# The first tile's loads split by heads on two queues, with filling transposes and weight conversions planned later

## The chip, the cores and the metric

The kernel runs on one core of a Trainium2 chip, in one launch. The metric is the device time of an execution in microseconds (us), and lower is better. The engines are TensorE (PE in the profile), VectorE (DVE), ScalarE (ACT), GpSimd (POOL) and SyncE (SP), which issues transfers.

## What is computed

Windowed causal attention with a linear bias by distance, then a mixer with a token part and a channel part, then a normalized channel part. Shapes: 4 batches, 8 heads, 576 positions, head size 64, so 2304 rows of 512.

```python
scores = q @ k.T / 8 + slope * -|i - j|, only where 0 <= i - j < 128
x = softmax(scores) @ v                          # rows of 512 (8 heads x 64)
u = x + (relu(x.T @ w_tok1) @ w_tok2).T          # w_tok1: 576 x 256
x = u + relu(u @ w_ch1) @ w_ch2                  # 512 x 1536, 1536 x 512
xn = (x - mean(x)) / sqrt(var(x) + 1e-6) * g_ln
out = x + relu(xn @ w2_ch1) @ w2_ch2             # 512 x 2048, 2048 x 512
```

q, k, v are given in f32. The weights arrive as 8-byte floats, which the kernel converts itself.

## The kernel before

The rows are cut into 18 tiles of 128 positions, over all batches. In the attention, each tile's scores are made in two groups of four heads (c = 0 and 1, L592), against the keys of the tile itself and of the tile before. A group goes through VectorE (L637: bias and minimum), ScalarE (L646: exp and sum), a transpose on TensorE (L653), a copy on ScalarE and masks on GpSimd (L361, L663); then the values (L608) and `normalize` (L667) give 128 rows of `u`. The token part (`tok1`, L694, and `tok2`, L722) runs beside the attention of later tiles. After the attention come two layers of channel products. In each, a first group of 8 row tiles, a group of 2 and a second group of 8 go through steps of 256 hidden columns: first products into the tiles b (L993 to L995) and, one step later, second products into acc (L1048 to L1050), added to `u` by VectorE (L1053).

Weights are read by `load_f64` (L381). One row of 8-byte floats is loaded twice, as the halves `rh` (one buffer) and `rw` (two buffers). ScalarE makes `e` from `rh` (L416), VectorE makes `s` (L419, L421), `m` (L423) and the f32 value, `y` or `w` (L431). Matrices used in products are then split into a high and a low part, on ScalarE and on GpSimd or VectorE (L374). Inside `attention()` there are 21 such loads: five of `wt1` and four of `wt2` (the token weights) and twelve of channel weights, of which six go to the `w` buffers and six to DRAM for later (`stage_w`). The other weights are loaded while the channel layers run.

The program's order isn't that of the code. Each operation is recorded with `op`: its costs by engine, what it reads and writes. `Plan.ranks` (L189) gives each a due time, counted back from its readers through waiting times (`LAT`) and twice the costs; a buffer that is used again links its old operations to the new ones. `Plan.order` (L205) then runs a list schedule in which all transfers are one engine, "DMA", and an engine that is free takes the ready operation that is due first. The instructions are written out in the order of the planned starts, and each engine and each queue works them off in that order. All transfers are issued by SyncE, but for the three of `shift_wt1` (L543).

At the start, ten pairs of transposes of the identity (`spin`, L757) keep TensorE busy (WARM = 10). Tile 0 is loaded as one transfer of keys (L532), one of q (L534, through L353) and one of its bias table (L767), each 256 KB. The two groups of tile 0's scores are chained: nothing is put between them, and the first waits for what both need.

Of the kernel before, what the change touches and what calls it, by code (L numbers as in the profile page):

```python
# [23 lines left out]
B, H, S, D = 4, 8, 576, 64  # L24
P = 128
DM = H * D
# [6 lines left out]
RING = 4  # L33
# [9 lines left out]
X_SHIFT, STAGE_SHIFT = -20, -20  # L43

STAGE_RATES = {(0, 2): 2, (1, 0): 2}
WARM, WARM_NS = 10, 320
WT_SHIFT, WT_START, WT_STEP, SHIFT_AT, W_START, W_STEP = 0, 2, 1, 7, 12, 2
SIGN16, EXP16 = 0x80008000 - (1 << 32), 0x7F807F80


# [52 lines left out]
class Plan:  # L103
# [11 lines left out]
    HOLD_ANY = False  # L115
    AHEAD = 2000
    SPARE = {"DVE": 1200, "ACT": 0}
    LAT = {"PE": 400, "DVE": 260, "ACT": 290, "POOL": 180, "DMA": 4000, "CTL": 0}

    def __init__(self):  # L120
        self.pools, self.ops, self.rings, self.ctl = {}, [], {}, {}
# [189 lines left out]
def pe(n):  # L311
    return 2.6 + n / 2.4


def block_kernel(tc, qT, kT, v, wt1, wt2, wa1, wa2, wb1, wb2, g, bias, out):
    nc = tc.nc
# [64 lines left out]
    def load_f64(src, k, n, dst=None, get=None):  # L381
# [25 lines left out]

        load_half(rh, at)
        load_half(rw, at + 3)

        def half(x):
            return x.t[:, :n].bitcast(I32)
# [49 lines left out]
    src = {"a1": wa1, "a2": wa2, "b1": wb1, "b2": wb2}  # L462
    wtiles, staged = [], {}
    used = [0]

    def convert_w(x, dst=None, get=None):

# [61 lines left out]
    def load_qk(i):  # L529
        r = i % RING  # L530
        b = qs[i] = buf("att", [P, H // 2, P], F32, "q", Q_BUFS)
        op({"DMA": 1000}, lambda: nc.sync.dma_start(out=keys.t[:, r].rearrange("p h t -> p (h t)"), in_=kT[i]),  # L532
           writes=[(keys, r)])
        load(b, lambda: b.t.rearrange("p h t -> p (h t)"), P * DM * 4, qT[i])  # L534

    def load_v(i):
        b = vs[i] = buf("atb", [P, H, D], F32, "v", 3)
# [40 lines left out]
    def packed(i, i2):  # L578

        parts, ready = [], []
        if i is not None:
            tiles, own, table, (a0, a1, a2) = keys_of(i)
            w = len(tiles) * P
            x = qs[i]
            for c in range(2):
                ps_t[i, c] = buf("psa", [P, 2, 2, 2 * P], F32, "ps_s", 2)  # L590

                def scores(c=c, ps=ps_t[i, c]):  # L592
                    for p in range(2):
                        for j in range(2):
                            r = slice(j * D, (j + 1) * D)
                            nc.tensor.matmul(ps.t[:, j, p, :w], x.t[r, 2 * c + p], keys.t[r, a0:a1:a2, 2 * c + p],  # L596
                                             start=True, stop=True)

                parts.append((4 * pe(2 * w), scores, [x] + [(keys, t % RING) for t in tiles], [ps_t[i, c]]))
        if i2 is not None:  # L600
            tiles2 = keys_of(i2)[0]
            na = len(tiles2)
            for c in range(2):
                def values(c=c, pf=pf_t[i2, c]):
                    for p in range(2):
                        for a, kt in enumerate((i2, i2 - 1)[:na]):
                            for j in range(2):
                                nc.tensor.matmul(pv.t[j * D:(j + 1) * D, 2 * c + p], vs[kt].t[:, 4 * c + 2 * p + j],  # L608
                                                 pf.t[:, a, 2 * p + j], start=(a == 0), stop=(a == na - 1))

                parts.append((na * 440, values, [(pf_t[i2, c], a) for a in range(na)] + [vs[kt] for kt in tiles2],
                              [(pv, c)]))

        before = None
        for k, (cost, emit, reads, writes) in enumerate(parts):
            also = parts[k + 1:] if k == 0 else []
            now = op({"PE": cost + (200 if k in (0, len(parts) - 1) else 0)}, emit,
               reads + [x for p in also for x in p[2]], writes + [x for p in also for x in p[3]])
            if before is not None:
                pl.chain[before] = now  # L620
            before = now

    def softmax(i, c):
# [12 lines left out]
        for m in range(4):  # L636
            op({"DVE": 358}, lambda m=m: nc.vector.tensor_tensor_reduce(  # L637
                out=t.t[:, m], in0=ps.t[:, m % 2, m // 2, o], in1=bias_sb.t[:, table, 4 * c + m],
                scale=-0.125, scalar=3.0e38, op0=ALU.add, op1=ALU.min, accum_out=mn.t[:, m:m + 1]),
               [ps, (bias_sb, table)], [(t, m), (mn, m)])  # L640
        pr = buf("att", [P, 4, P], F32, "pr", T_BUFS)
        if c == 0:
            rs_t[i] = buf("small", [P, H, 1], F32, "rs", 3)
# [103 lines left out]
    def attention():  # L747
# [15 lines left out]
        for _ in range(WARM):  # L763
            op({"PE": WARM_NS}, spin, [ident], [busy])
        pl.shift = 0
        def load_bias(a, b):
            op({"DMA": (b - a) * P * P * H * 2 / 360}, lambda: nc.sync.dma_start(  # L767
                out=bias_sb.t[:, a:b], in_=bias[:, a:b]), [], [(bias_sb, j) for j in range(a, b)])

        load_qk(0)  # L770
        load_bias(0, 1)
        load_qk(1)
        load_bias(1, 2)
        load_v(0)
# [10 lines left out]
        for i in range(-1, NTILE + 1):  # L785
            i0, i2 = i + 1 if i + 1 < NTILE else None, i - 1 if i > 0 else None
            if i0 is not None or i2 is not None:
                packed(i0, i2)
            if i >= 0 and i + 3 < NTILE:
                load_qk(i + 3)  # L790
            if 0 < i and i + 1 < NTILE:
# [9 lines left out]
            for c in range(2):  # L801
# [7 lines left out]
                elif r == 0 and 5 <= m < 9:  # L809
                    load_wt2(m - 5)  # L810
                pl.shift = 0
                if n == 1:
                    load_bias(2, 4)
                    load(g_sb, lambda: g_sb.t.rearrange("p k o -> p (k o)"), P * DM // P * 4, g)
                if n == SHIFT_AT:
                    shift_wt1()
# [264 lines left out]
    def swap(close=(), open_=()):  # L1081
# [6 lines left out]

        pl.control(emit, close, [n for n, _ in open_])

    rest = attention()

# [118 lines left out]
```

## Time and profile before

| | us |
|---|---|
| median of 3 runs | 855.08 |
| lowest and highest | 854.54, 855.89 |
| the profiled execution | 856.19 |
| its span, first to last instruction | 854.5 |

| engine | busy us | share of the span |
|---|---|---|
| TensorE matmul | 830.8 | 97% |
| VectorE | 638.1 | 75% |
| ScalarE | 394.3 | 46% |
| GpSimd | 338.5 | 40% |

The chain of work that ended last is TensorE for 83% and VectorE for 7% of the span. The mean granted TensorE clock is 0.996 of full. Times in the profile are from the span's start; matmuls are pipelined, so a stretch counts as busy from the first to the end of the last. Tiles are named as in the program.

### The profile page before, as it was taken

How to read it: one execution, taken by the hardware profiler on the slowest of the kernel's cores; microseconds unless marked ns; L12 is line 12 of the kernel's file. 1: busy time of each engine (PE TensorE's matmuls, PEld its weight loads, DVE VectorE, ACT ScalarE, POOL GpSimd, SP SyncE). 2: the span in 40 equal slices, each digit the busy share in tenths (PEclk: the TensorE clock that was granted, in tenths of full speed). 3: DMA queues.
4: the chain of work that ended last, by engine and by line, in shares of the span. 5: the costliest groups of instructions: out<-in, count | busy, mean ns of one | idle time of the engine just before them, and what ended most of it. 6: DMA issues, size and time to landing. Idle time of an engine off the chain costs nothing.

```text
span 854.5 us, 13205 instructions
## 1 busy us (share of the span) xinstructions
PE 830.8 (97%) x4478; PEld 685.8 (80%) x4478; DVE 638.1 (75%) x1311; ACT 394.3 (46%) x952; POOL 338.5 (40%) x353
## 2 busy tenths in 40 slices
PE   7999999979999999999999999999999999999997
PEld 6777888758888887788887888788889888888885
DVE  5787777987887989987888956988676855555554
ACT  6888766643434535334357323336357422222220
POOL 2685445554433556532235524614234612221110
PEclk9999999999999999999999999999999999999999
DMA  8678736457677699978762521887477762221112
GB/s 296 187 207 265 242 103 213 146 179 241 200 234 240 228 324 337 348 252 268 264 210 74 178 92 48 264 263 258 154 259 234 247 198 74 74 75 49 50 50 98
DMA packets 73698, 164.96 MB, mean 193 GB/s; under 512 B 8352, under 2 KB 8480, under 8 KB 73632
## 3 DMA queue, kind: packets, MB, share of 16 engines
q1 hardware_dynamic: 73152, 162.83, 57.5%
q0 software_dynamic: 480, 1.31, 0.7%
q8 instruction: 35, 0.57, 0.3%
q14 instruction: 31, 0.25, 0.1%
HBM read 131.34 MB, written 31.46 MB: 191 GB/s over the span
## 4 chain that ended last, share of the span: by engine, by line
PE 83%; DVE 7%; ACT 4%; DMA 2%; issue 2%; POOL 1%; SPq 1%; ACTq 0%; DVEq 0%; POOLq 0%
PE acc L1048 12%; PE acc L1050 12%; PE acc L1049 12%; PE b L993 9%; PE b L995 9%; PE b L994 9%; PE ps_v L608 3%; PE ps_s L596 3%; PE p L848 1%; PE b L442 1%; PE b L441 1%; PE b L440 1%; PE ps_t L653 1%; DVE st L374 1%; PE tok L735 1%
## 5 line engine op out<-in xcount | busy, mean ns | idle before, releaser
L1053 DVE TENSOR_TENSOR u<-acc,u 128x512 f32<-128x512 f32 x252 | 172.9, 687 | 64.0 <-PE acc L1050 60.6
L1048 PE MATMUL acc<-w2h,hh 128*128 128x512 f32 x504 | 198.6, 394 | 5.3 <-DVE u L1053 4.7
L1050 PE MATMUL acc<-w2h,hl 128*128 128x512 f32 x504 | 196.6, 390 | 0.3 <-DVE hl L926 0.2
L1049 PE MATMUL acc<-w2l,hh 128*128 128x512 f32 x504 | 196.5, 390 | 0.0
L924 ACT ACTIVATE hh<-b 128x512 fp32r<-128x512 f32 (+1 forms) x140 | 74.5, 552 | 262.8 <-PE b L995 226.4
L993 PE MATMUL b<-xh,w1h 128*128 128x512 f32 x392 | 154.0, 393 | 3.6 <-DVE hl L926 3.4
L994 PE MATMUL b<-xl,w1h 128*128 128x512 f32 x392 | 153.3, 391 | 1.8 <-DVE xl L374 1.8
L995 PE MATMUL b<-xh,w1l 128*128 128x512 f32 x392 | 153.4, 391 | 0.2 <-DVE w1l L374 0.2
L926 DVE SCALAR_TENSOR_TENSOR hl<-b,hh 128x512 fp32r<-128x512 f32 (+1 forms) x140 | 85.8, 631 | 62.9 <-ACT hh L924 62.1
L374 POOL TENSOR_TENSOR w1l<-w,w1h 128x512 fp32r<-128x512 f32 (+1 forms) x53 | 67.6, 1275 | 134.0 <-ACT w1h L361 124.2
L1048 PEld LDWEIGHTS acc<-w2h,hh 128*128 128x128 f32 x504 | 94.7, 188 | 27.0 <-DVE u L1053 7.5
L1050 PEld LDWEIGHTS acc<-w2h,hl 128*128 128x128 f32 x504 | 94.6, 188 | 21.2 <-DVE hl L926 1.2
L1049 PEld LDWEIGHTS acc<-w2l,hh 128*128 128x128 f32 x504 | 94.7, 188 | 18.4
L374 POOL TENSOR_TENSOR w1l<-st,w1h 128x512 fp32r<-128x512 f32 x38 | 51.1, 1346 | 116.5 <-ACT w1h L361 103.2
L993 PEld LDWEIGHTS b<-xh,w1h 128*128 128x128 f32 x392 | 73.9, 189 | 19.8 <-DVE hl L926 3.8
L994 PEld LDWEIGHTS b<-xl,w1h 128*128 128x128 f32 x392 | 74.0, 189 | 17.4 <-DVE xl L374 2.3
L995 PEld LDWEIGHTS b<-xh,w1l 128*128 128x128 f32 x392 | 73.9, 189 | 16.1 <-DVE w1l L374 0.6
L416 ACT ACTIVATE e<-rh 128x512 bf16<-128x512 bf16 (+2 forms) x65 | 41.3, 635 | 74.0 <-DMA rh<-wb 33.6
L646 ACT ACTIVATE pr<-t,mn 128x128 f32<-128x128 f32 x144 | 55.9, 392 | 15.1 <-DVE mn L637 14.9
L663 POOL TENSOR_SCALAR_AFFINE_SELECT pf<-pf 128x512 f32<-128x512 f32 x64 | 42.3, 661 | 37.7 <-ACT pf L361 35.5
L374 DVE TENSOR_TENSOR b<-b,p 128x512 f32<-128x512 f32 x56 | 39.0, 697 | 23.6 <-PE b L995 23.1
L374 POOL TENSOR_TENSOR w2l<-w,w2h 128x512 fp32r<-128x512 f32 x23 | 32.1, 1395 | 46.1 <-ACT w2h L361 46.0
(118 smaller groups left out, 1369.3 us busy)
## 6 DMA issues: line engine op xcount, KB each, us to landing
w<-d SPq DMA_DIRECT2D x88, 256.0 KB, 4.6
rw<-wb SPq DMA_DIRECT2D x32, 512.0 KB, 4.5
rh<-wb SPq DMA_DIRECT2D x32, 512.0 KB, 4.7
rw<-wa SPq DMA_DIRECT2D x24, 512.0 KB, 4.5
rh<-wa SPq DMA_DIRECT2D x24, 512.0 KB, 4.5
d<-y SPq DMA_DIRECT2D x32, 256.0 KB, 4.4
keys<-kT SPq DMA_DIRECT2D x18, 256.0 KB, 4.3
q<-qT SPq DMA_DIRECT2D x18, 256.0 KB, 4.7
```

The lines of the kernel that those rows point to most:

```text
L374: pl.op({e: cost[e] for e in on}, lambda e: ENGINE[e].tensor_tensor(get(), ga(), gb(), alu), [*several(a), *several(b), *also], several(dst))
L646: op({"ACT": 580}, lambda m=m: nc.scalar.activation(out=pr.t[:, m], in_=t.t[:, m], func=AF.Exp, bias=mn.t[:, m:m + 1], scale=-1.0, accum_o ...
L663: op({"POOL": 630}, lambda a=a: nc.gpsimd.affine_select(pf.t[:, a], pf.t[:, 1], [[0, 4], [1 - 2 * a, P]], (ALU.is_ge, ALU.is_gt)[a], 0.0, ...
L924: op({"ACT": act(n, True)}, lambda: nc.scalar.activation(out=hh.t[:, c], in_=go(), func=AF.Relu), [o], [(hh, key)])
L926: mark[0] = op({"DVE": dve(n)}, lambda: nc.vector.scalar_tensor_tensor(out=hl.t[:, c], in0=go(), scalar=0.0, in1=hh.t[:, c].bitcast(F32), ...
L993: nc.tensor.matmul(g.t, wh.t[:, w], xh.t, start=start and k == 0, stop=False, skip_group_check=True)
L994: nc.tensor.matmul(g.t, wh.t[:, w], xl.t, start=False, stop=False, skip_group_check=True)
L995: nc.tensor.matmul(g.t, wl.t[:, w], xh.t, start=False, stop=stop and k == 1, skip_group_check=True)
L1048: nc.tensor.matmul(o.t, hh.t[:, c:c + P], wh.t, start=j == 0, stop=False)
L1049: nc.tensor.matmul(o.t, hh.t[:, c:c + P], wl.t, start=False, stop=False)
L1050: nc.tensor.matmul(o.t, hl.t[:, c:c + P], wh.t, start=False, stop=j == 1)
L1053: op({"DVE": dve(DM)}, lambda o=o, i=i: nc.vector.tensor_tensor(u[i].t, o.t, u[i].t, ALU.add), [o], [u[i]])
```

## The change

Tile 0's keys, q and bias are each loaded as two halves of four heads; the halves of q are issued by ScalarE, the rest by SyncE. Tile 0's two score groups are no longer chained, and each waits for its own half. Seven warming pairs of transposes stand at the start instead of ten, and five more pairs read the second score buffer of tile 0, so they stand behind its scores, and the next user of that buffer (the scores of tile 1) stands behind them. In the planner, each raw weight load recorded in `attention()` has an operation of cost 1 on an engine "LATE" between the transfer and its readers, with a waiting time of 5000 ns; it issues no instruction. Some places in the program's record move: the token weights and `shift_wt1` by one step, the bias tables 2 and 3 by four.

```diff
-WARM, WARM_NS = 10, 320
-WT_SHIFT, WT_START, WT_STEP, SHIFT_AT, W_START, W_STEP = 0, 2, 1, 7, 12, 2
+LATE_NS = 5000
+WARM, WARM_NS, FILL = 7, 320, 5
+WT_SHIFT, WT_START, WT_STEP, SHIFT_AT, W_START, W_STEP = 0, 3, 1, 8, 12, 2
...
-    LAT = {"PE": 400, "DVE": 260, "ACT": 290, "POOL": 180, "DMA": 4000, "CTL": 0}
+    LAT = {"PE": 400, "DVE": 260, "ACT": 290, "POOL": 180, "DMA": 4000, "CTL": 0, "LATE": LATE_NS}
...
         load_half(rh, at)
         load_half(rw, at + 3)
+        if late[0]:
+            op({"LATE": 1}, lambda: None, [rh], [rh])
+            op({"LATE": 1}, lambda: None, [rw], [rw])
...
     def load_qk(i):
         r = i % RING
         b = qs[i] = buf("att", [P, H // 2, P], F32, "q", Q_BUFS)
+        if i == 0:
+            for c in range(2):
+                h, x = slice(2 * c, 2 * c + 2), slice(c * DM // 2, (c + 1) * DM // 2)
+                op({"DMA": 500}, lambda h=h, x=x: nc.sync.dma_start(
+                    out=keys.t[:, r, h].rearrange("p h t -> p (h t)"), in_=kT[i][:, x]), writes=[(keys, (r, c))])
+                op({"DMA": 100}, lambda h=h, x=x: nc.scalar.dma_start(
+                    out=b.t[:, h].rearrange("p h t -> p (h t)"), in_=qT[i][:, x]), writes=[(b, c)])
+                load_bias(0, 1, c)
+            return
...
+    def load_bias(a, b, c=None):
+        h = slice(0, H) if c is None else slice(4 * c, 4 * c + 4)
+        op({"DMA": (b - a) * P * P * (h.stop - h.start) * 2 / 360}, lambda: nc.sync.dma_start(
+            out=bias_sb.t[:, a:b, h], in_=bias[:, a:b, h]), [],
+           [(bias_sb, (j, x)) for j in range(a, b) for x in range(2) if c in (None, x)])
...
-                parts.append((4 * pe(2 * w), scores, [x] + [(keys, t % RING) for t in tiles], [ps_t[i, c]]))
+                parts.append((4 * pe(2 * w), scores, [(x, c)] + [(keys, (t % RING, c)) for t in tiles], [ps_t[i, c]]))
...
-            also = parts[k + 1:] if k == 0 else []
+            also = parts[k + 1:] if k == 0 and i != 0 else []
...
-            if before is not None:
+            if before is not None and i != 0:
                 pl.chain[before] = now
...
+            if i == -1:
+                for _ in range(FILL):
+                    op({"PE": 220}, spin, [ident, ps_t[0, 1]], [busy])
...
+                if n == 5:
+                    load_bias(2, 4)
                 if n == 1:
-                    load_bias(2, 4)
                     load(g_sb, lambda: g_sb.t.rearrange("p k o -> p (k o)"), P * DM // P * 4, g)
...
+    late[0] = True
     rest = attention()
+    late[0] = False
```

## Rows read from the trace of the kernel before

**Rows 1.** The page's first part: busy us, share of the span and instructions

```profile
PE 830.8 (97%) x4478; PEld 685.8 (80%) x4478; DVE 638.1 (75%) x1311; ACT 394.3 (46%) x952; POOL 338.5 (40%) x353
```

**Rows 2.** Busy time by stretch: length, engines' busy us, granted clock, DMA share, GB/s

```profile
core 0: us, PE busy (x) PEld busy (x) DVE busy (x) ACT busy (x) POOL busy (x), PEclk, DMA share, GB/s
7.20:15.00 7.80, 6.78 (x60) 4.97 (x60) 6.57 (x42) 6.83 (x32) 0.48 (x2) 1.00 1.04 390
...
19.00:22.00 3.00, 3.00 (x15) 2.31 (x16) 2.02 (x4) 2.59 (x12) 1.85 (x4) 0.50 0.55 122
...
30.00:140.00 110.00, 108.08 (x976) 86.21 (x973) 84.12 (x347) 87.17 (x306) 64.75 (x95) 1.00 0.67 201
156.00:184.00 28.00, 21.44 (x97) 16.49 (x96) 27.72 (x38) 15.02 (x27) 17.80 (x15) 0.98 0.41 132
188.00:290.00 102.00, 101.94 (x460) 84.16 (x459) 82.00 (x137) 42.90 (x80) 39.63 (x34) 1.00 0.67 222
```

**Rows 3.** Timeline of SyncE's queue: start us, us, line, transfer issued

```profile
0.79 0.39 SPq L532 DMA_DIRECT2D keys<-kT  x1
1.24 0.42 SPq L353 DMA_DIRECT2D q<-qT  x1
...
2.65 0.43 SPq L353 DMA_DIRECT2D q<-qT  x1
...
9.28 0.33 SPq L404 DMA_DIRECT2D rh<-wt  x1
```

**Rows 4.** DMA issues at 0.79, 1.24, 2.65 us: size, us to landing

```profile
keys<-kT SPq DMA_DIRECT2D x1, 256.0 KB, 2.8
...
q<-qT SPq DMA_DIRECT2D x1, 256.0 KB, 3.0
...
q<-qT SPq DMA_DIRECT2D x1, 256.0 KB, 4.5
```

**Rows 5.** Timeline of TensorE, 0 to 30 us

```profile
1.41 4.25 PE L759 MATMUL tok<-ident 128*128 128x128 f32 x20 [1.41 <-POOL ident masks.py:199]
5.59 1.16 PE L596 MATMUL ps_s<-keys,q 64*128 64x128 f32 x16
7.34 2.00 PE L596 MATMUL ps_s<-keys,q 64*128 64x256 f32 x16 [0.59 <-DVE mn L637]
...
19.17 3.53 PE L596 MATMUL ps_s<-keys,q 64*128 64x256 f32 x16
```

**Rows 6.** Timeline of VectorE and ScalarE, 0 to 22 us

```profile
2.08 0.20 ACT L754 ACTIVATE warm<-warm 128x1 f32<-128x1 f32 x1
...
6.36 0.29 DVE L637 CUSTOM_DVE_ANT_0 t<-ps_s,bias_sb 128x128 f32<-128x128 f32 x1 [5.44 <-PE ps_s L596]
...
15.25 0.43 ACT L416 ACTIVATE e<-rh 128x256 bf16<-128x256 bf16 x1 [1.14 <-DMA rh<-wt]
```

**Rows 7.** Groups of VectorE, 156 to 184 us: count, busy us, mean ns

```profile
L431 DVE SCALAR_TENSOR_TENSOR y<-m,s 128x512 f32<-128x512 uint32 x3 | 4.1, 1367 | 0.0
L423 DVE TENSOR_SCALAR m<-rw 128x512 uint32<-128x512 uint32 x3 | 2.9, 956 | 0.0
L421 DVE SCALAR_TENSOR_TENSOR s<-e,s 128x256 int32<-128x256 int32 x3 | 2.4, 811 | 0.0
L419 DVE TENSOR_SCALAR s<-e 128x256 int32<-128x256 int32 x3 | 1.4, 456 | 0.0
```

**Rows 8.** Timeline of ScalarE: conversions of channel loads 13, 16, 22 and 24

```profile
181.52 0.67 ACT L416 ACTIVATE e<-rh 128x512 bf16<-128x512 bf16 x1 [2.31 <-DVE s L421]
...
217.55 0.67 ACT L416 ACTIVATE e<-rh 128x512 bf16<-128x512 bf16 x1 [1.73 <-DVE s L421]
...
254.39 0.68 ACT L416 ACTIVATE e<-rh 128x512 bf16<-128x512 bf16 x1
...
270.73 0.66 ACT L416 ACTIVATE e<-rh 128x512 bf16<-128x512 bf16 x1 [2.53 <-DVE s L421]
```

**Rows 9.** Timeline of TensorE: first accumulations of steps 4 and 5

```profile
274.83 0.49 PE L1048 MATMUL acc<-w2h,hh 128*128 128x512 f32 x1
...
295.88 0.48 PE L1048 MATMUL acc<-w2h,hh 128*128 128x512 f32 x1
```

More of the change, by code (lines that the diff above doesn't have):

```diff
@@ L464, in block_kernel @@
     used = [0]
+    late = [False]
     def convert_w(x, dst=None, get=None):
@@ L531, in load_qk @@
         b = qs[i] = buf("att", [P, H // 2, P], F32, "q", Q_BUFS)
+        if i == 0:
[7 more added lines that the diff above has]
+            return
         op({"DMA": 1000}, lambda: nc.sync.dma_start(out=keys.t[:, r].rearrange("p h t -> p (h t)"), in_=kT[i]),
-           writes=[(keys, r)])
+           writes=[(keys, (r, c)) for c in range(2)])
         load(b, lambda: b.t.rearrange("p h t -> p (h t)"), P * DM * 4, qT[i])
+    def load_bias(a, b, c=None):
[3 more added lines that the diff above has]
+           [(bias_sb, (j, x)) for j in range(a, b) for x in range(2) if c in (None, x)])
     def load_v(i):
@@ L639, in softmax @@
                 scale=-0.125, scalar=3.0e38, op0=ALU.add, op1=ALU.min, accum_out=mn.t[:, m:m + 1]),
-               [ps, (bias_sb, table)], [(t, m), (mn, m)])
+               [ps, (bias_sb, (table, c))], [(t, m), (mn, m)])
         pr = buf("att", [P, 4, P], F32, "pr", T_BUFS)
@@ L765, in attention @@
         pl.shift = 0
-        def load_bias(a, b):
-            op({"DMA": (b - a) * P * P * H * 2 / 360}, lambda: nc.sync.dma_start(
-                out=bias_sb.t[:, a:b], in_=bias[:, a:b]), [], [(bias_sb, j) for j in range(a, b)])
         load_qk(0)
-        load_bias(0, 1)
         load_qk(1)
```

## The prediction

> **What bounds the kernel now.** I read the page first: TensorE is busy for 97% of the span [rows 1], so what can be won is its idle time, its time at the lower clock, and nothing else. Busy time by stretch then shows where that is. From 30 to 140 us TensorE is busy 108.08 of 110 us, and from 188 to 290 us 101.94 of 102 [rows 2]: a microsecond lost or won before such a stretch goes through it unchanged, and nothing is to be won within it. Two places are left. One is the front, up to about 23 us. The other is the change from attention to the first channel layer, 156 to 184 us, where VectorE is busy 27.72 of 28 us and TensorE only 21.44: 6.56 us are idle there, behind VectorE.
>
> In the front I read three things. SyncE issues the first transfers one after the other, from 0.79 us on [rows 3]. They are 256 KB each. Keys and q of tile 0 land at 0.79+2.8 = 3.6 and 1.24+3.0 = 4.2 us, and the q of tile 1, fifth in line behind the bias of tile 0 and the keys of tile 1, at 2.65+4.5 = 7.2 [rows 3, 4]: issues are 0.45 us apart, landings on average 0.9, so the transfers limit. On TensorE [rows 5] the first scores follow the warming transposes at 5.59 us though their data is there at 4.2, so the spins hold them; the first reduce starts at 6.36 [rows 6]. The scores of tile 1 start at 7.34, right behind the landing of its q at 7.2. Later ScalarE waits 1.14 us for a token weight in front of the conversion at 15.25 [rows 6]; after that, in 19 to 22 us, TensorE's granted clock is 0.50, the 1.2 GHz level [rows 2]: 16 score matmuls then take 3.53 us, against 2.00 at 7.34 [rows 5].
>
> **The change, part by part.** *Which load is first.* The planner gives the free transfer slot to the load with the earliest due time, counted backwards from TensorE's work; it is a sorting key, not a time on the chip. All raw weight loads share one buffer "rh", so each is chained to the one after it. One link of a token weight counts 2·728+4000+2·400+290 = 6.5 us back in the old kernel. The 21 loads built inside the attention (9 token, 12 channel) now each have a "LATE" step between transfer and conversion, 5000 ns and twice its cost of 1, so 5.0 us more. By the old kernel's costs the first keys are due at -88.0 us and the first rh at -36.2. The change takes 21·5.0 = 105 us off the latter: -141. Likewise the first two "rw" loads go from -27 and -21 to about -122 and -111. The halves of tile 0 stay near -86. So I expect three 256 KB token loads, issued 15th and later before (the rh at 9.28, [rows 3]), at the head of SyncE's queue, with tile 0 behind them.
>
> *Tile 0.* Its keys and q are then complete as the fifth 256 KB in line, which lands at 7.2 us today [rows 4]: the first scores at 7.2 instead of 5.59, +1.6. The two q halves are issued by ScalarE behind its table warm-up at 2.08 us, two issues of about 0.42 as SyncE's are; ScalarE has nothing else until the first reduce at 6.36 ends [rows 3, 6], so this costs nothing; without that cover 0.8. The busy share of the 16 DMA engines is 1.04 from 7.2 to 15 us at 390 GB/s [rows 2], so the q halves count in the line whoever issues them. Were the second queue a second path, the line would be 256 KB, or 0.67 us, shorter: +0.9. The Trainium skill ("DMA: Bandwidth & Descriptors", section "Issuing engines are not separate DMA queues") says that transfers started by different engines run on the same 16 and save only time of issue; by that rule it is +1.6 and by two paths +0.9, and the saturated row agrees with the rule.
>
> *Spins and fill.* Three fewer warming pairs are 6·4.25/20 = 1.3 us less: the spins end at 1.41+14·0.2125 = 4.4 us [rows 5]. That is worth nothing while tile 0 comes later. The five filling pairs are 10·0.2125 = 2.1 us, and they sit in front of tile 1's scores, which wait for them as readers of the score buffer. So tile 1's scores start at 7.2+1.16+2.1 = 10.5 instead of 7.34: +3.1. If the scores come at 4.4, the fill lies in a wait for q of tile 1 and is free. What comes back is the 1.14 us wait of ScalarE, because that weight now lands first, and the 3.53-2.00 = 1.5 us of the slow scores, if the clock holds: -2.7. The front is +0.4. Bounds: -2.3 (scores at 4.4, and ScalarE's wait gone) and +4.6 (nothing comes back, and the 2.8 us gap before the scores puts one score group at 1.2 GHz, 3.1+1.5).
>
> *Order of conversions.* A channel weight's link was 1456+4000+631+290 = 6.4 us of the plan and is now 11.4. Today three conversions fall into the 28 us in which VectorE is the limit, each 1.37+0.96+0.81+0.46 = 3.6 us of VectorE [rows 7]. At the longer spacing 3·6.4/11.4 = 1.7, so about one fewer: -3.6, less than the 6.56 us that TensorE idles there. Bounds: 0 (none leaves) and -6.6. The conversions are not gone. By the new links the attention's 21 loads end at 231 us of the plan (next step), where the old plan has them done at about 190; (231-190)/11.4 is about four conversions that come after the change of phases instead of before. That is four times 3.6 = 14 us more for VectorE from 188 to 290 us, where it has 102-82 = 20 free [rows 2]; this hides them, and without it up to 14 us would show.
>
> *Weights in the channel layer.* The price is that the later weights start late. The new links come to 5·10.4+4·10.5+12·11.4 = 231 us. The 13th channel load, converted at 181.52 today [rows 8], moves back by somewhat under 41 us; I take 36, to 217.5. From there loads can follow at (254.39-217.55)/6 = 6.1 us, as today's seven conversions from one to the other do [rows 8]. The 24th is then at 217.5+11·6.1 = 284.6, and with 5.7 us to its use (conversion 0.7, VectorE about 3, split 2) it is there at 290.3, before the accumulation that starts at 295.88 [rows 9]. The 22nd, at 272.4+5.7 = 278.1, is late for the accumulation at 274.83 [rows 9] by 3.3 us; other products can go first, so I take +1.0. Bounds: 0, and +8 where that lateness returns at each of two or three steps.
>
> *The rest.* Moving the other bias tables and the shift by one or two places in the program changes no due time. The bias tables have no use before tile 4, whose scores start after 19 us [rows 5], and cost nothing; issued later than today, their 512 KB would stand behind loads that have time. The tile's bias in two halves is the same bytes.
>
> **Sum.** +0.4-3.6+1.0 = -2.2 us. The profiled execution took 856.19 us, 854.5 of it the span; the runs' median is 855.08, 1.1 below it, within 0.13%. I take the difference off the median: 852.9 us.
>
> **The rivals.** (1) *Weights run short*, the one that ends slower. Place: the accumulations of steps 3 to 5, from about 254 us. Price: up to 8 us. It decides once the shift at the 13th load is more than the (295.88-270.73) = 25 us that today's last conversion has in hand [rows 8, 9] and what catching up gives back. With the front as above: 855.1+0.4-3.6+8 = 859.9. For it: TensorE has no idle time there to hide a wait [rows 2]. Against: the conversions of that stretch already wait in their queue today, so there is some room. (2) *The front costs its full bound*: +4.6-3.6+1.0, 857.1. For it: the fill stands in front of tile 1 in any case. Against: today's stalls at 15 to 22 us cannot be repeated for data that has landed. (3) *The change does what it says*: tile 0 stays first in line. Scores at 4.4 instead of 5.59 is -1.2, ScalarE's wait -1.1, with the later conversions -3.6 and +1.0: 850.2. Against it stands the chain of due times. (4) *One takes the other back*: the order of VectorE fills the vacated place with other conversions, gain and loss cancel, and the time stays at 855.1 within 1.7.
>
> **How the numbers follow.** 0.2%, 1.7 us, is about what a measurement of this kernel can tell from no change. The forecast has 0.32, rival 3 0.12: faster 0.44. Rival 4: same 0.24. Rival 1 0.20 and rival 2 0.12: slower 0.32. Below 848 and above 862 I leave the far ends, a transition gained in full with a quick front, or weights short by the full price with the front at its bound. The forecast alone spans 850 to 853.3.
>
> **What would show it.** Right: SyncE's first issues are rh and rw; first scores near 7.2 us, tile 1's near 10.5; no wait of ScalarE for rh before 20 us; two or fewer conversions on VectorE in the last 28 us of the change of phases, TensorE's idle time there near 3 us; the 13th channel conversion after 210 us. Wrong: keys first and scores at 4.4 (rival 3); TensorE waiting for w2h or w2l at 254 to 300 us (rival 1); clock 0.50 between 5 and 12 us (rival 2); as many conversions as today in the change of phases (rival 4).

## The result and the profile after

| | before | after |
|---|---|---|
| median (lowest to highest), us | 854.54 (851.94 to 855.89), 5 runs | 860.30 (858.58 to 863.56), 5 runs |
| span of the profiled execution, us | 854.5 | 860.1 |

The ratio of after to before is 1.0082, with a 95% interval of [1.0064, 1.0101]: the change costs about 0.8%. I forecast 852.9, faster. What happened is close to rival 1, for which I had worked out 859.9, and I had given it a chance of 0.20.

First the head of the queues. SyncE's timeline of the changed kernel (start, us, line, transfer) stands against [rows 3]:

```profile
0.79 0.38 SPq L405 DMA_DIRECT2D rh<-wt  x1
1.23 0.89 SPq L405 DMA_DIRECT2D rw<-wt  x2
2.16 0.91 SPq L542 DMA_DIRECT2D keys<-kT  x2
3.11 0.43 SPq L548 DMA_DIRECT2D keys<-kT  x1
3.59 1.69 SPq L554 DMA_DIRECT2D bias_sb<-bias  x2
6.03 0.33 SPq L354 DMA_DIRECT2D q<-qT  x1
```

Three token loads stand first, as derived from the due times; tile 0 is behind them. TensorE's timeline of the same stretch (start, us, in brackets the idle time before and what ended it) answers [rows 5], and the two lines after it, of VectorE and ScalarE, [rows 6]:

```profile
6.90 1.46 PE L618 MATMUL ps_s<-keys,q 64*128 64x128 f32 x16 [2.40 <-DMA keys<-kT]
8.29 2.40 PE L781 MATMUL tok<-ident 128*128 128x128 f32 x10
10.48 0.87 PE L675 MATMUL ps_t<-ident,pr 128*128 128x128 f32 x4
11.28 2.00 PE L618 MATMUL ps_s<-keys,q 64*128 64x256 f32 x16
...
22.43 2.00 PE L618 MATMUL ps_s<-keys,q 64*128 64x256 f32 x16
```

```profile
7.97 0.29 DVE L659 CUSTOM_DVE_ANT_0 t<-ps_s,bias_sb 128x128 f32<-128x128 f32 x1 [7.05 <-DMA bias_sb<-bias]
```

```profile
8.70 0.42 ACT L421 ACTIVATE e<-rh 128x256 bf16<-128x256 bf16 x1
```

Tile 0's scores wait for their keys, the first reduction waits for its bias, the fill comes next, then four transposes of tile 0's probabilities (10.48), and tile 1's scores start 3.94 us later than before. ScalarE's wait for rh is gone, and the scores of tile 3 (22.43) take 2.00 us instead of 3.53. Busy time by stretch answers [rows 2]:

```profile
7.20:15.00 7.80, 6.73 (x51) 5.64 (x47) 5.41 (x35) 5.50 (x23) 0.97 (x2) 0.78 0.99 345
19.00:22.00 3.00, 2.48 (x19) 1.38 (x15) 2.20 (x15) 2.58 (x10) 2.29 (x5) 1.00 0.75 243
30.00:140.00 110.00, 107.89 (x995) 87.40 (x991) 79.95 (x338) 85.04 (x307) 63.28 (x94) 1.00 0.63 189
156.00:184.00 28.00, 22.53 (x103) 17.37 (x102) 26.43 (x39) 14.14 (x26) 17.50 (x14) 0.96 0.39 116
188.00:290.00 102.00, 98.51 (x431) 80.07 (x430) 82.77 (x135) 42.01 (x78) 41.95 (x37) 0.98 0.71 228
```

The last line is the one that matters. In the channel layer, where TensorE had been busy for 101.94 us of 102 at full clock, it is now busy for 98.51 at 0.98: 3.4 us more are idle, and about 1.6 more are lost to the clock, which is at 0.60 for the 4 us from 256 (below). Conversions 13, 22 and 24 on ScalarE's timeline, against [rows 8], show what came later:

```profile
217.68 0.66 ACT L421 ACTIVATE e<-rh 128x512 bf16<-128x512 bf16 x1 [3.71 <-DMA rh<-wa]
...
277.75 0.69 ACT L421 ACTIVATE e<-rh 128x512 bf16<-128x512 bf16 x1
...
292.92 0.66 ACT L421 ACTIVATE e<-rh 128x512 bf16<-128x512 bf16 x1 [2.27 <-DMA rh<-wa]
```

The 24th comes 22 us later than before, and the first accumulation of step 5 starts at 301.64 instead of 295.88 [rows 9]. How that reaches TensorE is seen in ScalarE's queue:

```profile
251.82 1.09 ACT L946 ACTIVATE hh<-b 128x512 fp32r<-128x512 f32 x2 [2.55 <-PE b L1017]
252.79 0.63 ACT L362 ACTIVATE w1h<-st 128x512 fp32r<-128x512 f32 x1
253.31 0.42 ACT L362 ACTIVATE w1h<-w 128x256 fp32r<-128x256 f32 x1
253.62 0.60 ACT L362 ACTIVATE p<-b 128x512 f32<-128x512 f32 x1
254.09 0.64 ACT L362 ACTIVATE w2h<-w 128x512 fp32r<-128x512 f32 x1
254.61 0.61 ACT L362 ACTIVATE b<-b 128x512 f32<-128x512 f32 x1
```

and on TensorE right after:

```profile
252.75 0.39 PE L1017 MATMUL b<-xh,w1l 128*128 128x512 f32 x1
255.28 0.50 PE L1015 MATMUL b<-xh,w1h 128*128 128x512 f32 x1 [2.13 <-ACT b L362]
...
257.17 0.63 PE L1071 MATMUL acc<-w2l,hh 128*128 128x512 f32 x1
257.59 0.63 PE L1072 MATMUL acc<-w2h,hl 128*128 128x512 f32 x1
...
279.28 0.50 PE L1015 MATMUL b<-xh,w1h 128*128 128x512 f32 x1 [0.82 <-ACT b L362]
282.84 0.50 PE L1015 MATMUL b<-xh,w1h 128*128 128x512 f32 x1 [0.54 <-DVE b L375]
```

TensorE doesn't wait for a weight here. It waits until a first product is moved out of its accumulator (b<-b at 254.61), and that copy stands in ScalarE's queue behind three splits of late weights. This step is read from the trace: no run moved the copy ahead of the splits. After the wait the granted clock falls, as TensorE's busy time by stretch shows:

```profile
256.00:260.00 4.00, 4.00 (x13) 3.14 (x12) 1.98 (x5) 0.00 (x0) 0.00 (x0) 0.60 0.94 256
```

The eight products from 256.77 to 260.15 start 0.42 us apart instead of 0.23, so the 2.13 us cost about 1.6 more.

A table of milestones shows where time goes in each kernel. Each entry is the start of the first matmul of its group on TensorE's timeline, as after minus before, in us.

| | before at | after | front_only | late_only | late_channel | late_token | delay |
|---|---|---|---|---|---|---|---|
| scores of tile 0 | 5.59 | +1.31 | -0.55 | +1.58 | +0.52 | -1.00 | +4.05 |
| scores of tile 1 | 7.34 | +3.94 | +0.10 | +3.18 | +2.56 | +0.47 | +4.05 |
| scores of tile 2 | 11.20 | +5.14 | +0.10 | +6.24 | +3.27 | +1.68 | +4.04 |
| scores of tile 17 | 125.81 | +1.55 | +2.26 | +8.93 | +8.78 | +1.75 | +5.25 |
| first acc, step 0 | 191.93 | -0.79 | +2.29 | +2.33 | +0.66 | +0.16 | +5.29 |
| first acc, step 2 | 233.23 | -0.90 | +2.26 | +2.10 | +0.51 | +0.05 | +5.28 |
| first acc, step 5 | 295.88 | +5.76 | +2.25 | +6.18 | +0.47 | +0.03 | +5.28 |
| first acc behind the wait for `u` | 467.48 | +4.27 | +2.32 | +4.49 | +0.48 | +0.07 | +5.35 |
| last acc | 849.28 | +5.83 | +2.28 | +4.51 | +0.49 | +0.07 | +5.36 |

So after is 1.55 us late by the last scores, gives 2.34 back in the change of phases, is 0.79 ahead at step 0, and loses 6.55 in steps 3 to 5. Of that 1.49 come back until the wait for `u`, a wait of 1.9 us that every kernel has. In after the granted clock falls behind this wait (0.66 from 471 to 476 us) and 1.56 us are lost again; in the kernel before it doesn't fall (1.00 from 466 to 476). TensorE's lines there, before and after:

```profile
467.48 0.50 PE L1048 MATMUL acc<-w2h,hh 128*128 128x512 f32 x1 [1.91 <-DVE u L1053]
```

```profile
471.75 0.75 PE L1070 MATMUL acc<-w2h,hh 128*128 128x512 f32 x1 [1.92 <-DVE u L1075]
```

late_to4, a run that loses nothing in steps 3 to 5, has the same fall there (0.72 from 466 to 472 us). So the late weights cost about 5.1 us, and the fall of 1.56 is not shown to be theirs.

Each column is one execution. That of the kernel before took 856.19 us, 1.1 to 1.8 above the medians of its runs, and that of delay was the slowest of its ten. So differences of some 2 us between a last row and a median mean little: by the medians late_channel is 2.75 us slower, late_token 0.74 and delay 3.29.

### The profile page after: what moved, and what is told of

The parts are those of the page before. It is cut to its first block, busy times and chain, and to the rows that moved or that the text cites. A ratio compares the mean times of both kernels' runs of the same rounds, so it can differ in the third digit from the quotient of the medians.

```text
span 860.1 us, 13215 instructions
## 1 busy us (share of the span) xinstructions
PE 834.3 (97%) x4482; PEld 688.9 (80%) x4482; DVE 633.2 (74%) x1307; ACT 392.1 (46%) x952; POOL 340.5 (40%) x357
## 3 DMA queue, kind: packets, MB, share of 16 engines
q0 software_dynamic: 480, 1.31, 0.8%
## 4 chain that ended last, share of the span: by engine, by line
PE 88%; DVE 5%; ACT 3%; DMA 2%; issue 1%; POOL 0%; SPq 0%; DVEq 0%; ACTq 0%
PE acc L1070 13%; PE acc L1071 13%; PE acc L1072 13%; PE b L1015 10%; PE b L1017 10%; PE b L1016 10%; PE ps_v L630 3%; PE ps_s L618 3%; PE p L870 2%; PE b L447 2%; PE b L446 2%; PE b L445 2%; PE ps_t L675 1%; DVE st L375 1%; PE tok L757 1%
## 5 line engine op out<-in xcount | busy, mean ns | idle before, releaser
L946 ACT ACTIVATE hh<-b 128x512 fp32r<-128x512 f32 (+1 forms) x140 | 74.5, 552 | 269.8 <-PE b L1017 225.7
L375 POOL TENSOR_TENSOR w1l<-w,w1h 128x512 fp32r<-128x512 f32 (+1 forms) x52 | 64.4, 1240 | 157.3 <-ACT w1h L362 147.9
L375 POOL TENSOR_TENSOR w1l<-st,w1h 128x512 fp32r<-128x512 f32 x40 | 54.4, 1363 | 115.2 <-ACT w1h L362 107.1
L375 DVE TENSOR_TENSOR b<-b,p 128x512 f32<-128x512 f32 x56 | 39.0, 697 | 22.2 <-PE b L1017 21.7
L362 ACT ACTIVATE w1h<-w 128x512 fp32r<-128x512 f32 x84 | 46.2, 555 | 7.1 <-issue 3.5
```

What stands on the lines that cost most here:

```text
L362: nc.scalar.activation(out=get(), in_=gsrc(), func=AF.Copy, scale=scale)
L375: pl.op({e: cost[e] for e in on}, lambda e: ENGINE[e].tensor_tensor(get(), ga(), gb(), alu), [*several(a), *several(b), *also], several(dst))
L946: op({"ACT": act(n, True)}, lambda: nc.scalar.activation(out=hh.t[:, c], in_=go(), func=AF.Relu), [o], [(hh, key)])
```

## The experiments

The theory after the result is that weights run short: the twelve channel loads, planned later, leave a backlog that is paid for in steps 3 to 5. Its rivals are that the front costs the time, and that each late link costs its share wherever it is. Ratios are to runs of the kernel before on the same chip.

**Each half alone.** front_only is the changed kernel without the links, late_only the kernel before with nothing but the links.

```diff
-    late[0] = True
     rest = attention()
-    late[0] = False
```

> The changed kernel without the LATE steps: halves of tile 0, seven warming and five filling pairs stay. Two theories are to be told apart. 'Weights short' says the loss (scores 5.8 us late from step 5 on) comes from the channel loads' longer links, which leave the weights of steps 3 to 5 late. 'Front' says it comes from what is done to the first two tiles (halves, fill, fewer warming pairs). With normal links the first loads are keys again. Weights short: step 3 to 5 as in the kernel before, first scores near 4.4 us, total 853 to 854.5. Front: the loss stays, 858 to 861.

Measured: 858.14 us, ratio 1.0037 [1.0020, 1.0053]. The time lies in the range of 'front', but the loss that was to be explained isn't there: steps 3 to 5 lose nothing, as weights short had it. The front itself loses 2.3 us, which neither theory had: tile 0's scores at 5.05 bring tile 1's nothing, since they wait for the next load, and the first weight conversion then stands in ScalarE's queue for longer, with TensorE idle behind it and at half clock after that. The conversion's line, and busy time by stretch:

```profile
15.89 0.43 ACT L421 ACTIVATE e<-rh 128x256 bf16<-128x256 bf16 x1 [1.67 <-DMA rh<-wt]
```

```profile
15.00:19.00 4.00, 1.14 (x8) 0.84 (x8) 2.46 (x12) 2.12 (x7) 1.27 (x2) 0.93 0.90 297
19.00:22.00 3.00, 2.31 (x10) 1.62 (x12) 2.87 (x14) 3.00 (x15) 1.27 (x2) 0.50 0.74 263
22.00:25.00 3.00, 3.00 (x18) 2.01 (x16) 1.00 (x2) 1.71 (x6) 2.50 (x5) 0.50 0.28 95
```

> The kernel before with the LATE steps alone: tile 0 whole on SyncE's queue, ten warming pairs, no fill. Weights short: 13th channel conversion near 217 us, TensorE waits at 250 to 290 us, total 859 to 861 like the changed kernel. Front: at most the delay of tile 0 by three token loads, which is made good by 192 us as in the changed kernel: 854 to 856.

Measured: 859.91, 1.0078 [1.0057, 1.0099], as weights short had it. The links alone make nearly the whole loss. Its place is only in part that of the changed kernel: of 4.5 us at the last accumulation 2.3 stand at step 0 already, and 2.2 come behind it.

**Which links.** The condition on the link is changed, the rest is the changed kernel.

```diff
-        if late[0]:
+        if late[0] and n == DM:     # late_channel
+        if late[0] and n != DM:     # late_token
```

> The changed kernel with the LATE steps on the twelve channel loads only, not on the nine token loads. The token loads are quick again, so the chain of loads gets to the 13th channel load about as early as in the kernel before (202 instead of 198 us of the plan), though the channel loads keep their long links; token loads still come first in the queue. Weights short: no wait at 250 to 290 us, 853 to 856. Front: tile 0 stays behind token loads and the fill stays, so 858 to 861. A third, 'each late link costs wherever it is': about half of the loss or more, 858 to 860.

Measured: 857.16, 1.0041 [1.0028, 1.0054], between the ranges, and no loss in steps 3 to 5: its 13th conversion stands at 192.3. Where the 2.75 us of the medians are lost the trace doesn't show, since its execution is only 0.49 late at the end. The twelve channel links alone don't make the weights late; it takes the nine token links ahead of them in the same chain of buffers.

> The changed kernel with the LATE link on the token stage's nine loads alone, so that no channel load is modelled with it. The first loads in SyncE's order are then the keys of tile 0 again, and the 13th load conversion should stand near 181 us as in the kernel before (there 181.52). Theory 'weights short': without the twelve late channel loads nothing is lost in steps 3 to 5 (the first acc of step 5 no later against step 0 than before). Theory 'wait for rh' for the front: what the front part alone lost (2.27 us, behind ScalarE's 1.67 us wait for rh at 15.89 us and a spell at clock 0.50) came from the first rh landing late, and with that load ahead both go: together 851.5 to 854.5 us. Rival 'the front itself' (the fill and the order of tile 1's loads cost whatever rh does): the loss of some 2 us stays, 855.5 to 858.

Measured: 855.34, 1.0015 [1.0004, 1.0026], between the ranges. Steps 3 to 5 lose nothing (+0.16 at step 0, +0.03 at step 5), as weights short had it. The front's wait for rh is gone too, but the gain that I expected with it isn't there. TensorE and VectorE show a new wait in its place:

```profile
12.88 3.57 PE L618 MATMUL ps_s<-keys,q 64*128 64x256 f32 x16 [1.14 <-DMA q<-qT]
```

```profile
6.80 0.29 DVE L659 CUSTOM_DVE_ANT_0 t<-ps_s,bias_sb 128x128 f32<-128x128 f32 x1 [5.88 <-DMA bias_sb<-bias]
```

Tile 0's scores start at 4.59, and then the first reduction waits for the bias until 6.80, which is later than the 6.36 of the kernel before [rows 6].

**How many.** The link on the token loads and on the first 4, or the first 8, of the twelve channel loads.

```diff
-        if late[0]:
+        if n == DM:
+            channel[0] += 1
+        if late[0] and (n != DM or 1 <= channel[0] <= 4):     # or 8
```

> The changed kernel with the LATE link on the token loads and on only the first four channel loads (instead of twelve): a smaller dose. 'Weights short': the 13th load conversion stands some 6 us later than in the kernel before (187 to 190 instead of 217.7 in the changed one), and the loss in steps 3 to 5 falls from 6.6 us to between 0 and 1.5; with the front's loss of 0 to 2: 854 to 858. Rival 'each late link costs wherever it is': 13 of 21 links, thus 13/21 of the changed kernel's loss of 5.8, 857.5 to 859.

Measured: 855.94, 1.0009 [0.9997, 1.0020]; nothing is lost in steps 3 to 5. The rival of equal shares falls with it.

> The changed kernel with the LATE link on the token loads and the first eight channel loads (twelve in the changed kernel, four in an earlier run that lost nothing in steps 3 to 5). 'Weights short' as a stock that runs out: the 13th load conversion between 195 and 208 us; steps 3 to 5 lose nothing while it is before some 195 and up to 6.5 us at 217, so 0 to 3 us here, and with the changed kernel's front (rh and two rw ahead of the keys) 855 to 859. 'Each late link costs': 17 of 21 links, 4.7 us of 5.8, 859 to 860.

Measured: 858.80, 1.0045 [1.0028, 1.0062]. The time agrees with both, the place only with the first: steps 3 to 5 lose nothing. Of 4.0 us at step 0, 2.3 come from the front and 1.7 from the change of phases. TensorE is idle there for as long as in the kernel before (busy for 21.54 us against 21.44), but its clock is lower, 0.88 against 0.98 [rows 2], behind a wait for VectorE. The wait, and busy time by stretch:

```profile
177.15 0.61 PE L1018 MATMUL b<-xl,w1h 128*128 128x512 f32 x1 [3.56 <-DVE xl L375]
```

```profile
156.00:184.00 28.00, 21.54 (x97) 17.07 (x97) 27.15 (x36) 14.94 (x28) 21.52 (x17) 0.88 0.44 150
```

The doses in one table, from ScalarE's and TensorE's timelines (us):

| kernel | 13th conversion | 24th | last scores to step 0 | step 0 to step 5 | step 0 to behind the wait for `u` |
|---|---|---|---|---|---|
| before | 181.5 | 270.7 | 66.11 | 103.96 | 275.55 |
| front_only | 183.9 | 273.0 | 66.14 | 103.92 | 275.58 |
| late_token | 183.6 | 270.8 | 64.52 | 103.84 | 275.47 |
| late_to4 | 188.0 | 269.8 | 64.41 | 103.82 | 275.42 |
| late_channel | 192.3 | 271.2 | 58.00 | 103.76 | 275.37 |
| late_to8 | 199.9 | 274.7 | 67.82 | 103.88 | 275.52 |
| after | 217.7 | 292.9 | 63.78 | 110.50 | 280.61 |
| late_only | 221.4 | 292.8 | 59.52 | 107.80 | 277.71 |
| no_fill | 222.0 | 295.2 | 63.93 | 109.33 | 279.42 |
| late_not_due | 237.4 | 312.1 | 60.89 | 134.76 | 303.96 |

Steps 0 to 5 take 103.8 to 104.0 us for every shift of the 13th conversion up to 18.4 us, 3.8 to 6.5 more at 36 to 41, and 30.8 more at 56. A part comes back: by the last column the price is 2.2 to 5.1 us at 36 to 41, and 28.4 at 56. It is a stock: lateness is free until it is used up. The start of step 5 says so too: its first accumulation starts 25.1 us after the 24th conversion in every kernel that loses nothing there, and 8.7 to 9.4 us after it in the four that do, however late it is. There the supply sets the pace. The last scores to step 0 don't follow the lateness; the order does that (below).

**More lateness.** The link counts where the plan is laid out, but not in the due times.

```diff
-        return 0 if e == "PE" and e2 == "PE" else self.LAT[e] + self.TO_PE * (e2 == "PE")
+        return 0 if e == "PE" and e2 == "PE" else (0 if e == "LATE" and self.ranking else self.LAT[e]) + self.TO_PE * (e2 == "PE")
...
+        self.ranking = True
...
+        self.ranking = False
```

> The changed kernel in which the LATE steps keep their 5000 ns in the list schedule but count nothing in the due times. Tile 0 is first in the queue again (front as in front_only), but the loads wait behind other work as well as behind the late steps: the 13th channel conversion stands at 269 us of the plan instead of 242. Weights short: TensorE waits far more at steps 1 to 5, 875 to 895. Front: 853 to 856, since the first tiles are not delayed.

Measured: 882.53, 1.0334 [1.0308, 1.0360]. The time is in the range of weights short. The keys are first, tile 0's scores are 1.00 us early, and the loss is in steps 1 to 5 alone. With this much lateness TensorE waits for the weights themselves (waits of TensorE, 188 to 300 us: line, what it waited for, us, times, longest):

```profile
PE acc L1072 <- ACT w2h L364: 6.8, 1, 6.8
PE b L1017 <- ACT w1h L364: 6.5, 2, 4.8
```

**Does a delay in the front go through?** late_only and late_channel are 8.9 and 8.8 us late at the last scores, but only 2.3 and 0.7 at step 0. Here the kernel before gets forty more transposes in its last warming pair, and the order of everything else stays as it was.

```diff
+        spun = [0]
...
+            spun[0] += 1
-            for _ in range(2):
+            for _ in range(42 if spun[0] == WARM else 2):
                 nc.tensor.transpose(busy.t[:, :P], ident.t, ident.t)
```

> The kernel before, with forty more transposes of the identity in its last warming pair and the order of everything else exactly as it was: TensorE starts its scores about 8.5 us later (some 14.1 us instead of 5.59), and nothing else is changed. It tells what becomes of a delay in the front, since two kernels that were 8.8 to 8.9 us late at the last scores were only 0.5 and 2.3 us late at the first accumulation. 'Goes through', the claim of the prediction: what the front doesn't give back by itself (up to 2.7 us, the wait for rh and the slow scores) stands at the last scores and at the first accumulation alike, 860 to 863.5 us. 'The change of phases has slack of its own': the lateness at the last scores shrinks by more than half until the first accumulation, whatever the order, 855.5 to 858.5. If it goes through, it was the order of the conversions in those two kernels that gave the time back, not the lateness.

Measured: 858.38, 1.0033 [1.0020, 1.0046]. The delay is smaller than I had sized it (4.05 us instead of 8.5). In the profiled execution it goes through to the last accumulation whole, with 1.2 us more from the front. So there the change of phases has no slack of its own, and what gave the time back in the other two was their order, not their lateness. The median alone wouldn't decide: it lies in the range that I had set for slack, but both ranges were for 8.5 us. With 4.05 they would be 856.4 to 859.1 for going through and 855.1 to 857.1 for slack. What the faster executions gave back, and where, no trace shows.

VectorE finished three channel values from 156 to 184 us in the kernel before [rows 7], and two in late_channel, in the changed kernel and in late_only (the line of late_channel):

```profile
L436 DVE SCALAR_TENSOR_TENSOR y<-m,s 128x512 f32<-128x512 uint32 x2 | 1.9, 930 | 0.0
```

From the last scores to step 0, a stretch that moves along with the kernel, it is eight values before and five in these three and in no_fill. The count isn't all of it: late_token and late_to4 give 1.6 and 1.7 us back there with eight and nine. TensorE, 6.6 us idle from 156 to 184 us before, is busy for nearly all of it in late_channel, at a clock of 1.00 instead of 0.98:

```profile
156.00:184.00 28.00, 26.74 (x132) 21.57 (x131) 26.78 (x41) 15.82 (x29) 17.64 (x15) 1.00 0.31 93
```

**The fill.** FILL = 0, the order of the rest unchanged.

```diff
-WARM, WARM_NS, FILL = 7, 320, 5
+WARM, WARM_NS, FILL = 7, 320, 0
```

> The changed kernel without the ten filling transposes; the order of everything else is the same. In the changed kernel they run from 8.29 to 10.70 us, while TensorE would wait for the first tile's probabilities. 'Covered': no difference, 859 to 861.5. 'The fill keeps the clock': a longer spell at half clock without it, 861.5 to 864. 'The fill is in the way': tile 1's scores come earlier by 0.5 to 2 us and it goes through, 857.5 to 859.

Measured: 862.01, 1.0087 [1.0073, 1.0102], against 1.0082 [1.0064, 1.0101] with the fill. The fill is not in the way. The time lies in the range of 'the fill keeps the clock', but whether the fill helps by the 1.1 us between the two last accumulations can't be told from these intervals; it moves the stretch at a low clock. With it TensorE is at 0.50 from 8 to 10 us, while the fill runs; without it at 0.55 from 19 to 22:

```profile
19.00:22.00 3.00, 3.00 (x22) 2.12 (x20) 2.22 (x7) 1.72 (x8) 2.15 (x4) 0.55 0.39 124
```

**What the split front is worth.** Three kernels with the links on the token loads alone: the old front; the new one with tile 0 loaded whole, its q by ScalarE; and the new one with tile 0's bias ahead of tile 1's keys.

```diff
     # before_late_token: the kernel before, with this (and LATE in LAT) alone
+        if late[0] and n != DM:
+            op({"LATE": 1}, lambda: None, [rh], [rh])
+            op({"LATE": 1}, lambda: None, [rw], [rw])
...
     # three_loads, in place of the halves
+            op({"DMA": 1000}, lambda: nc.sync.dma_start(
+                out=keys.t[:, r].rearrange("p h t -> p (h t)"), in_=kT[i]), writes=[(keys, (r, c)) for c in range(2)])
+            op({"DMA": 200}, lambda: nc.scalar.dma_start(
+                out=b.t.rearrange("p h t -> p (h t)"), in_=qT[i]), writes=[(b, c) for c in range(2)])
+            load_bias(0, 1)
...
     # bias_first
+                pl.shift = -146.3
                 load_bias(0, 1, c)
+                pl.shift = 0
```

> The kernel before with the LATE link on the token stage's nine loads alone; the front is the old one. rh comes sixth in SyncE's order instead of later. 'Wait for rh': ScalarE's 1.14 us wait at 15.25 us goes and the half-clock scores at 19.17 us with it, 852 to 854. Rival 'each late link costs': a loss of 1 to 4 us, 855.5 to 858.5. If it is as fast as the changed front with the same links, the split loads of tile 0 bring nothing.

Measured: 853.90, 0.9990 [0.9980, 1.0001]. That is in the first range, but not told apart from no change.

> The changed kernel with LATE on the token loads alone, and with the first tile loaded whole again: keys and bias in one transfer each on SyncE's queue, q in one on ScalarE's; the fill and the seven warm-up steps stay. Theory 'ring of eight': in the trace the ninth transfer of the program waits on the semaphore of the first, the tenth on that of the second and so on, so the three extra transfers of the halves use up the ring and hold SyncE's queue (in the run with halves from 4.49 to 6.30 us), and tile 2's q comes late (1.14 us wait and half-clock scores at 12.88 us). With whole loads that pause goes: tile 2's scores at 11.0 to 11.7 us instead of 12.88, no wait for q there, and the last acc 2 to 3.5 us earlier than in the run with halves; 852 to 853.9. Rival 'bias late': the loss comes from tile 0's bias standing behind tile 1's keys; the same order of whole loads as in the kernel before cures that too, and the run with bias first (beside this one) should then be as fast. Rival 'fill and warm-up': the loss stays, 855 to 857.

Measured: 854.51, 0.9996 [0.9984, 1.0008], between the ranges. Tile 2's scores start at 11.33 without a wait for q, as 'ring of eight' had it, but the last accumulation comes only 1.2 us before that of late_token.

> The changed kernel with LATE on the token loads alone and the halves kept, but tile 0's two bias halves ahead of tile 1's keys on SyncE's queue. 'Bias late': the first reduction, which waited for the bias until 6.80 us, starts at 5.9 to 6.4, and the loss of some 2 us against the old front goes, 852.5 to 854. 'Ring of eight': as many transfers as with the halves before, the ninth waits still; the first reduction may start sooner but tile 2's scores stand at 12.3 us or later, 854.5 to 856.

Measured: 855.67, 1.0010 [0.9998, 1.0021]: by its time the range of 'ring of eight', by its trace that of 'bias late'. Its first reduction starts at 5.87 and the scores of tile 2 at 11.66, with as many transfers as late_token:

```profile
5.87 0.29 DVE L661 CUSTOM_DVE_ANT_0 t<-ps_s,bias_sb 128x128 f32<-128x128 f32 x1 [4.95 <-PE ps_s L620]
```

```profile
11.66 2.00 PE L620 MATMUL ps_s<-keys,q 64*128 64x256 f32 x16
```

So their number alone doesn't make tile 2 late. That the bias does isn't shown either. With the bias moved SyncE also stands still for 0.9 us instead of 1.8 (waiting for an earlier landing, in both runs), and tile 2's q is issued at 6.22 instead of 7.14. And in late_not_due the first reduction starts at 6.99, later than in late_token, and tile 2's scores still start at 11.87, without a wait. What made them late in late_token is the wait for q.

In the profiled executions of the three the last accumulation comes 2.8, 1.1 and 2.4 us earlier than in that of the kernel before; the medians say 0.7 and 0.4 faster, and 0.8 slower. Executions of one kernel differ by more than that (bias_first from 853.58 to 856.80), and why its profiled one was its fastest is open. None of the three beats the kernel before by more than a measurement tells; the best, before_late_token, has only the earlier token loads and the old front.

## Why the prediction was wrong

**Which load is first: right.** rh and two rw came first, 256 KB each, as the due times said.

**Tile 0: right in its mechanism but for one term, and the size was off within the bounds.** Scores at 6.90 (forecast 7.2), tile 1's at 11.28 (10.5), the wait of 1.14 us and the slow scores gone. The difference at tile 1 is a term that I had left out: the four transposes of tile 0's probabilities, which stand between the fill and tile 1's scores (10.48 to 11.28, 0.80 us). The fill took 2.19 us to the next start, where I had said 2.1, and that was luck: it ran at a granted clock of 0.50 (8 to 10 us), behind the 2.40 us wait for the keys; in front_only, at 1.00, it took 1.3. The front was +1.55 by the last scores, where I had said +0.4, with bounds of -2.3 and +4.6. The two prices of a second queue, +1.6 and +0.9, aren't told apart by the measured +1.31, so the rule of the Trainium skill ("DMA: Bandwidth & Descriptors", section "Issuing engines are not separate DMA queues") stays undecided here. ScalarE issued q's halves at 0.96 us, not behind its warm-up; that changed nothing.

**Order of conversions: as forecast, the size within the bounds.** One fewer in the change of phases (two instead of three), and 2.34 us came back where I took 3.6. TensorE's idle time there fell only from 6.6 to 5.5 us, since one wait of 4.1 us for VectorE remained; where the other 1.2 us came from isn't traced. That the missing conversion is the cause isn't shown: late_token and late_to4 give 1.6 and 1.7 us back without one. The conversions not done by 188 us were four more, as worked out (9 instead of 13 had begun).

**Weights in the channel layer: the step that failed.** The term was +1.0 and measured 6.55 at step 5, of which 5.06 were left by the wait for `u`. The sum of -2.2 became 1.55-2.34+5.06 = +4.3, and the fall of the clock behind that wait made it +5.8. The shift was right: 217.5 forecast for the 13th conversion, 217.68 measured; there was some luck in it, since 36 was my choice below the 41 worked out, and late_only, with the same links, was shifted by 40. Three things behind it were not right.
- *The rate.* I took 6.1 us from one conversion to the next, the six of the kernel before that ran quickest. From the 16th to the 24th of that same kernel it is (270.73-217.55)/8 = 6.65 [rows 8], and after it was (292.92-217.68)/11 = 6.84. So the 24th came at 292.9 instead of 284.6, and with 5.7 us to its use (8.7 to 9.4 were measured in the late kernels) was past step 5's accumulation at 295.88 instead of ahead of it. The 22nd was late by 277.75+5.7-274.83 = 8.6, not 3.3.
- *The price of lateness.* "Other products can go first" looked at TensorE alone. As the trace shows it, the loss came through ScalarE, whose queue holds the splits of late weights and the copies of the step in one fixed order, and in the changed kernel with a stretch at half clock (late_only and no_fill lose without one).
- *My own rule.* I wrote that rival 1 decides once the shift is more than 25 us and what catching up gives back. The 25 us run from the last conversion's start to the accumulation and leave out the 5.7 to its use, so about 19.5 were in hand. And the six quick conversions made me count on 22 us of catching up, where 14 came: the 24th was 22.2 late, which is under 25 and over 19.5. The runs put the point between 18 and 36 us of shift. Its place was right and its price of up to 8 us nearly so; its form wasn't, since TensorE waited for w2h only in late_not_due.

**VectorE's 20 free us** from 188 to 290 were said to hide the four conversions. VectorE was busy 82.77 us there instead of 82.00, so it was not the limit. The 14 us more of work didn't come up either: 14 conversions began in the stretch, against 12 before.

**"Goes through unchanged": true of a delay, not of a kernel.** The profiled execution of the run with a pure delay shows it to the tenth of a microsecond from the last scores on. Where the order changed as well, up to 8.1 us were given back in the change of phases (late_channel, 66.11 to 58.00).

**Not tested.** The moves of the bias tables and of the shift were not run alone. A second rh buffer, which would test the rate directly, was not tried, nor the copy of a first product ahead of the splits.

## What to carry to other kernels

When a change makes a supply later, take the rate of catching up from its longest steady stretch and compare the lateness with the stock in hand; below the stock it cost nothing here, above it 2.2 to 28.4 us, and a mean over the two is nobody's price. Count the stock to the use, not to the conversion. Ask of late work not only who reads it but what stands behind it on its engine. And a first tile that starts earlier gains nothing by itself: late_token's scores started 1.00 us earlier, and its first reduction, which waited for the bias, 0.44 us later.

## What was not expected of the hardware

Forty more transposes of the identity took 4.05 us, 0.10 each, where I had counted 0.21 each from the twenty of the kernel before [rows 5]. In the run delay, whose whole stretch is this line of TensorE,

```profile
1.41 8.30 PE L762 MATMUL tok<-ident 128*128 128x128 f32 x60 [1.41 <-POOL ident masks.py:199]
```

single transposes start 0.21 us apart up to 4.45 us and 0.11 apart from there on. The trace's records of the granted clock begin at 4.59 us in this run, and at 5.25 in the kernel before, where the spacing changes at 5.28; a stretch ahead of the first record is printed as 1.00, which is no measurement. In the changed kernel the fill's transposes start 0.21 us apart at a recorded 0.50, and in front_only 0.11 apart at 1.00. So all but the last of the twenty ran at the slow spacing, and their row was no price for forty more behind them.

A short wait ahead of a dense stretch cost more than itself where the granted clock fell after it: 2.13 us became about 3.7 in the changed kernel at 255 us, and in front_only TensorE was busy for 1.14 of 4 us and then ran at 0.50, the 1.2 GHz level, from 19 to 25 us. Executions of that one kernel took from 853.43 to 859.76 us.
